# Token mixing of an attention-plus-MLP kernel moved from the second stage into the attention loop

## The chip, the cores and the metric

The kernel runs on one core of one Trainium2 chip. The metric is the device time of one execution in microseconds; the time before is 919.98 us, the median of five runs from 918.11 to 921.35.

In the profile PE is TensorE's matmul and PEld its weight load, DVE is VectorE, ACT is ScalarE, POOL is GpSimd, and SP is the engine that only issues DMAs.

## The reference

Windowed attention with eight global tokens, then a residual MLP with token mixing. Eight batches, eight heads, 576 tokens, 64 numbers per head, 512 per token.

```python
scores = scale * np.matmul(q, k.transpose(0, 1, 3, 2))
mask = np.abs(pos[:, None] - pos[None, :]) <= window          # window = 32
mask = mask | is_global[:, None] | is_global[None, :]
attn = softmax(np.where(mask, scores, -1e9))
x = heads_joined(np.matmul(attn, v))                          # (8, 576, 512)

a1 = alpha1 * x + beta1
tok = np.einsum('ts,bsd->btd', w_tok, a1)                     # token mixing
u = x + lam * tok
a2 = alpha2 * u + beta2
ch = np.maximum(a2 @ w_ch1, 0.0) @ w_ch2                      # 512 -> 2048 -> 512
return u + lam * ch
```

## The kernel before

A prologue loads and folds the weights: W1 and W2 (bf16, with alpha2 and lam inside), wtT, which is w_tok transposed, LA1 = alpha1 * lam and LB1 = beta1 * lam.

**Attention (L270 to L397)** loops over batches and, within each, over heads. Per head the tokens are the rows of q, k and v in five tiles of 128. TensorE transposes q and k into `trps`; VectorE copies them to `QT` and `KT`. `scps` takes the scores of nine 128 x 128 blocks of the band and of the global rows (L335, L340), ScalarE writes their Exp to `PT` (L351), VectorE multiplies `PT` by the mask (L352), and TensorE multiplies with v into `pvps` (L358, L363) and, for the global rows, into `scps` (L372). The 65th column of v is one, so the denominator comes out beside the result. VectorE copies `pvps` to `xstg` (L381, L383) and the denominator of the global rows to `xg` (L385). `vg_ext` (L329, L330) holds v of the global tokens for the head; the score matmuls write the same PSUM tile that it is read from and start behind it. PSUM tiles `scps`, `pvps` and `trps` have one buffer each; SBUF tiles have two. The transposes and copies of q and k run two heads ahead.

At a batch's end SP writes `xstg` to `x_dram` in DRAM (L390), and POOL adds the global rows there with an indirect DMA (L391).

**MLP (L407 to L464)** loops over batches. `X` is read from `x_dram`; VectorE divides it by the denominators (`rden`, L412, L415), makes `XL` = X * LA1 in bf16 (L418) and sets one extra row of it to LB1 (L419). For each of five token tiles, five matmuls of 512 columns with `wtT` make `tkps` (L427), and VectorE adds X to get `U` (L434). Four f32 transposes per tile (L441) go through `utps` to `UT` in bf16 (L442). Then come 128 matmuls of 288 columns into `hps` (L450), each four followed by a Relu on ScalarE into `HT` (L453), and 80 of 512 columns into `chps` (L459). VectorE adds U (L463), and SP stores the result (L464).

The order on each engine is set by a scheduler from priorities in the order of the code, and each engine runs its own list in order. SP issues all loads and stores but those of v and the indirect ones, which POOL issues; a DMA that waits holds up what stands behind it.

Of the kernel before, what the change touches and what calls it, by code (L numbers as in the profile page):

```python
# [67 lines left out]
def kernel(  # L68
# [144 lines left out]
    with tc.tile_pool(name="w_psum", bufs=1, space=bass.MemoryType.PSUM) as wpp:  # L213
        bps = wpp.tile([P, 16], FP32, name="bps")
        for ec in range(16):
            for cc in range(4):
# [33 lines left out]
        nc.vector.tensor_copy(out=wtT[64:65, 4, :], in_=rps[64:65, :])  # L250
    p0_cm.__exit__(None, None, None)

    with (
        tc.tile_pool(name="pG", bufs=2) as pG,
        tc.tile_pool(name="pStage", bufs=2) as pStage,
        tc.tile_pool(name="pA", bufs=2) as pA,
        tc.tile_pool(name="psA_sc", bufs=1, space=bass.MemoryType.PSUM) as psA_sc,
        tc.tile_pool(name="psA_pv", bufs=1, space=bass.MemoryType.PSUM) as psA_pv,
        tc.tile_pool(name="psA_tr", bufs=1, space=bass.MemoryType.PSUM) as psA_tr,
    ):  # L260
# [138 lines left out]
    with (
        tc.tile_pool(name="pB", bufs=2) as pB,  # L400
        tc.tile_pool(name="pBh", bufs=1) as pBh,
        tc.tile_pool(name="psB_tok", bufs=2, space=bass.MemoryType.PSUM) as psB_tok,
        tc.tile_pool(name="psB_h", bufs=2, space=bass.MemoryType.PSUM) as psB_h,
        tc.tile_pool(name="psB_ch", bufs=2, space=bass.MemoryType.PSUM) as psB_ch,
        tc.tile_pool(name="psB_tr", bufs=1, space=bass.MemoryType.PSUM) as psB_tr,
    ):
        for b in range(NBATCH):  # L407
            xd = x_dram[b]
            X = pB.tile([P, NT, XW], FP32, name="X")
            nc.sync.dma_start(out=X, in_=xd.rearrange("(t p) f -> p t f", p=P))  # L410
            rden = pB.tile([P, NT, 8], FP32, name="rden")
            nc.vector.reciprocal(out=rden, in_=X[:, :, DM:XW])  # L412
            rden_b = bass.AP(rden.tensor, rden.offset, [rden.ap[0], rden.ap[1], [1, 8], [0, 64]])
            Xn = X[:, :, 0:DM]
            nc.vector.tensor_tensor(out=Xn, in0=Xn, in1=rden_b, op=ALU.mult)  # L415
            XL = pB.tile([P, NT, DM], BF16, name="XL")
            LA1_b = bass.AP(LA1.tensor, LA1.offset, [LA1.ap[0], [0, NT], [1, DM]])
            nc.vector.tensor_tensor(out=XL, in0=Xn, in1=LA1_b, op=ALU.mult)  # L418
            nc.vector.tensor_copy(out=XL[64:65, 4, :], in_=LB1[64:65, :])  # L419

            U = pB.tile([P, NT, DM], FP32, name="U")
            for t in range(NT):
                tsz = P if t < 4 else 64
                tkps = psB_tok.tile([P, DM], FP32, name="tkps")
                for sc in range(NT):
                    ssz = P if sc < 4 else 65
                    nc.tensor.matmul(  # L427
                        out=tkps[0:tsz, :],
                        lhsT=wtT[0:ssz, sc, t * P : t * P + tsz],
                        rhs=XL[0:ssz, sc, :],  # L430
                        start=(sc == 0),
                        stop=(sc == 4),
                    )
                nc.vector.tensor_tensor(out=U[0:tsz, t, :], in0=tkps[0:tsz, :], in1=Xn[0:tsz, t, :], op=ALU.add)  # L434

            UT = pBh.tile([P, 4, S], BF16, name="UT")
            for t in range(NT):
                tsz = P if t < 4 else 64
                utps = psB_tr.tile([P, 4, P], FP32, name="utps")
                for cc in range(4):  # L440
                    nc.tensor.transpose(out=utps[:, cc, 0:tsz], in_=U[0:tsz, t, cc * P : (cc + 1) * P], identity=ident[0:tsz, 0:tsz])  # L441
                nc.vector.tensor_copy(out=UT[:, :, t * P : t * P + tsz], in_=utps[:, :, 0:tsz])  # L442

            HT = pBh.tile([P, 16, S], BF16, name="HT")
            for ec in range(16):
                for nn in range(2):
                    tsl = slice(0, 288) if nn == 0 else slice(288, S)
                    hps = psB_h.tile([P, 288], FP32, name="hps")
# [46 lines left out]
```

## Time and profile before

| | |
|---|---|
| median of five runs | 919.98 us |
| the profiled execution | 920.4 us |
| its span, first to last instruction | 918.6 us |
| granted TensorE clock, mean | 0.995 |
| TensorE busy | 725.5 us, 79% |
| VectorE busy | 347.5 us, 38% |
| ScalarE busy | 332.1 us, 36% |
| GpSimd busy | 155.5 us, 17% |
| DMA, mean | 90 GB/s |
| end of the attention stage | about 549 us |

Busy shares are means over stages with different limits, so the rows below go stage by stage. A timeline row gives where the instruction starts in the span and how long it ran; in brackets stands how long its engine was idle before it, and what ended that. PE rows overlap, since matmuls are pipelined; how far apart they start tells more than how long one is.

### The profile page before, as it was taken

Reading aid. Unit: us, or ns where it says so; the run is one execution under the profiler, and the core shown is the slowest. Engines: PE = TensorE matmul, PEld = TensorE weight load, DVE = VectorE, ACT = ScalarE, POOL = GpSimd, SP = SyncE. Lnnn points to the kernel's source line nnn. Section 1 sums busy time; section 2 is a strip of 40 time slices with the busy share of each in tenths; the row PEclk is TensorE's granted clock in tenths of the full one; section 3 lists DMA queues with packets and bytes.
Section 4 is the critical chain, followed back from the end, with each engine's and each line's share of the span. In section 5 each row is a group of like instructions: output and inputs, shape, how many; then the busy total and the mean of one; then the engine's idle time right before and its main releaser. Section 6 shows DMA issues by size and latency. Waiting matters only on the chain.

```text
span 918.6 us, 13166 instructions
## 1 busy us (share of the span) xinstructions
PE 725.5 (79%) x5054; PEld 448.2 (49%) x5091; DVE 347.5 (38%) x857; ACT 332.1 (36%) x641; POOL 155.5 (17%) x295
## 2 busy tenths in 40 slices
PE   0158777777777777777777761999999999999988
PEld 0125545545455455454554530556565656556554
DVE  2654333343334343334333324715243352613111
ACT  0014444434344444444444430334260615244251
POOL 0036233242332422422323200000000000000000
PEclk9999999999999999999999999999999999999989
DMA  4826343353433433434334104112113020200101
GB/s 133 342 70 151 90 136 90 88 139 84 126 103 82 136 90 87 139 89 135 90 88 134 39 16 159 59 47 64 55 57 110 12 99 24 87 35 18 46 6 52
DMA packets 114503, 82.83 MB, mean 90 GB/s; under 512 B 90248, under 2 KB 90776, under 8 KB 113928
## 3 DMA queue, kind: packets, MB, share of 16 engines
q1 hardware_dynamic: 106232, 62.60, 23.2%
q0 software_dynamic: 8208, 19.40, 7.1%
q8 instruction: 40, 0.66, 0.3%
q14 instruction: 23, 0.19, 0.1%
HBM read 61.75 MB, written 20.22 MB: 89 GB/s over the span
## 4 chain that ended last, share of the span: by engine, by line
PE 72%; DVE 15%; DMA 7%; issue 3%; ACT 2%; SPq 0%; POOL 0%; POOLq 0%; DVEq 0%
PE chps L459 15%; PE hps L450 14%; PE scps L335 8%; PE pvps L363 8%; PE trps L320 5%; PE trps L317 5%; PE pvps L358 5%; PE tkps L427 3%; DVE QT L318 3%; PE pvps L348 3%; DVE KT L321 3%; DMA w2raw<-in_moe_w_ch_dram 3%; DVE xstg L381 3%; DMA X<-xdram 2%; PE pvps L347 2%
## 5 line engine op out<-in xcount | busy, mean ns | idle before, releaser
L453 ACT ACTIVATE HT<-hps,bias1T 128x288 bf16<-128x288 f32 x256 | 127.2, 501 | 224.5 <-PE hps L450 224.5
L459 PE MATMUL chps<-W,HT 128*128 128x512 bf16 (+1 forms) x611 | 152.0, 380 | 1.1 <-ACT HT L453 0.4
L450 PE MATMUL hps<-UT,W 128*128 128x288 bf16 x1024 | 149.1, 286 | 2.1 <-DVE UT L442 0.2
L450 PEld LDWEIGHTS <-W 128*128 128x128 bf16 x1024 | 99.7, 97 | 46.1 <-issue 21.0
L463 DVE TENSOR_TENSOR ob<-chps,U 128x512 f32<-128x512 f32 (+1 forms) x40 | 27.6, 690 | 203.0 <-PE chps L459 176.9
L351 ACT ACTIVATE PT<-scps 128x1192 f16<-128x1192 f32 x64 | 74.5, 1164 | 64.0 <-PE scps L340 64.0
L305 ACT CAST vext<-vn 128x320 f16<-128x320 f32 x64 | 29.3, 458 | 179.2 <-PE scps L372 177.9
L335 PE MATMUL scps<-QT,KT 64*128 64x128 bf16 x576 | 78.3, 285 | 19.0 <-DVE vg_ext L330 18.4
L459 PEld LDWEIGHTS <-HT 128*128 128x128 bf16 (+1 forms) x640 | 62.1, 100 | 63.4 <-issue 3.4
L358 PE MATMUL pvps<-vg_ext,pgc 8*128 8x65 f16 x320 | 73.9, 231 | 0.0
L317 PE MATMUL trps<-identb,qn 128*64 128x128 bf16 x320 | 44.6, 304 | 33.8 <-DVE KT L321 30.9
L363 PE MATMUL pvps<-voext,PT 128*128 128x65 f16 x448 | 71.1, 240 | 0.0
L427 PE MATMUL tkps<-XL,wtT 128*128 128x512 bf16 (+2 forms) x192 | 52.4, 394 | 23.3 <-DVE XL L418 21.5
L381 DVE COPY xstg<-pvps 128x320 f32<-128x320 f32 x64 | 31.5, 492 | 95.0 <-PE pvps L363 95.0
L320 PE MATMUL trps<-identb,kn 128*64 128x128 bf16 x320 | 44.5, 302 | 25.3 <-DVE QT L318 25.3
L318 DVE COPY QT<-trps 64x640 bf16<-64x640 bf16 x64 | 30.9, 483 | 85.1 <-PE scps L340 79.7
L264 POOL DMA_DIRECT2D vn<-in_v_dram x63 | 58.1, 922 | 28.2 <-ACT xg L384 24.1
L340 PE MATMUL scps<-qgT,KT 64*128 64x8 bf16 x320 | 62.5, 211 | 0.0
L317 PEld LDWEIGHTS <-qn 128*64 128x64 bf16 x320 | 39.2, 166 | 42.4 <-issue 42.0
L363 PEld LDWEIGHTS <-PT 128*128 128x128 f16 x576 | 40.7, 111 | 36.9 <-DVE PT L352 19.3
L335 PEld LDWEIGHTS <-KT 64*128 64x128 bf16 x576 | 55.4, 127 | 1.4 <-issue 1.4
L340 PEld LDWEIGHTS <-KT 64*128 64x128 bf16 x320 | 41.4, 129 | 28.2 <-issue 28.2
(94 smaller groups left out, 823.4 us busy)
## 6 DMA issues: line engine op xcount, KB each, us to landing
xdram<-xstg SPq DMA_DIRECT2D x8, 1300.0 KB
X<-xdram SPq DMA_DIRECT2D x8, 1300.0 KB
qn<-in_q_dram SPq DMA_DIRECT2D x63, 160.0 KB
kn<-in_k_dram SPq DMA_DIRECT2D x63, 160.0 KB
vn<-in_v_dram POOLq DMA_DIRECT2D x63, 160.0 KB
vo<-in_v_dram POOLq DMA_DIRECT2D x64, 128.0 KB
out_dram<-ob SPq DMA_DIRECT2D x32, 256.0 KB
w1raw<-in_moe_w_ch_dram SPq DMA_DIRECT2D x1, 4096.0 KB
```

Source lines behind the costliest of these rows:

```text
L317: nc.tensor.transpose(out=trps[:, c, :], in_=qn16[:, c, :], identity=identb)
L320: nc.tensor.transpose(out=trps[:, c, :], in_=kn16[:, c, :], identity=identb)
L335: nc.tensor.matmul(out=scps[:, bi * P : (bi + 1) * P], lhsT=KTf[:, c : c + P], rhs=QT[:, t, :], start=True, stop=True)
L340: nc.tensor.matmul(out=scps[:, GR_OFF + 8 * si : GR_OFF + 8 * si + 8], lhsT=KTf[:, c : c + P], rhs=qgT[:, 8 * h : 8 * h + 8], start=True, ...
L351: nc.scalar.activation(out=PT, in_=scps[:, 0:SCORE_F], func=AF.Exp, bias=0.0, scale=0.125)
L358: nc.tensor.matmul(out=pvps[:, t * PV_T : t * PV_T + PV_T], lhsT=pgc[:, gsl], rhs=vg_ext, start=True, stop=False)
L363: nc.tensor.matmul(out=pvps[:, t * PV_T : t * PV_T + PV_T], lhsT=PT[:, bi * P : (bi + 1) * P], rhs=rhs, start=False, stop=(ci == len(tbis) ...
L381: nc.vector.tensor_copy(out=xstg[:, :, D * h : D * h + D], in_=src_num)
L427: nc.tensor.matmul(out=tkps[0:tsz, :], lhsT=wtT[0:ssz, sc, t * P : t * P + tsz], rhs=XL[0:ssz, sc, :], start=(sc == 0), stop=(sc == 4),)
L450: nc.tensor.matmul(out=hps, lhsT=W1[:, cc, ec * P : (ec + 1) * P], rhs=UT[:, cc, tsl], start=(cc == 0), stop=(cc == 3))
L453: nc.scalar.activation(out=HT[:, ec, tsl], in_=hps, func=AF.Relu, bias=bias1T[:, ec : ec + 1], scale=1.0)
L459: nc.tensor.matmul(out=chps[0:tsz, :], lhsT=HT[:, ec, t * P : t * P + tsz], rhs=W2[:, ec, :], start=(ec == 0), stop=(ec == 15))
```

## The change

The token mixing, from the load of X to UT, leaves the MLP loop and becomes `emit_B1(batch, piece)`, eight pieces:
- piece 0 loads X and takes the reciprocal `rden`;
- piece 1 multiplies X by it and, new, runs two f32 matmuls of 512 columns (`warm`) whose result nobody reads;
- piece 2 makes XL and clears half a tile of U;
- pieces 3 to 7 each make one `tkps` and one tile of U; the last of them also transposes all of U to UT and writes U and UT to DRAM (`u_dram`, `ut_dram`).

Within head h of batch b the code now calls `emit_B1(b - 1, h)`; batch 7's eight pieces follow the loop. The MLP loop reads U and UT back from DRAM and starts with hps. `tkps` has one PSUM buffer instead of two. HT and UT get pools that are open from before the attention on.

```diff
+        def emit_B1(bb, piece):
+            if bb < 0:
+                return
+            st = b1st
+            if piece == 0:
+                st["X"] = pB1.tile([P, NT, XW], FP32, name="X")
+                nc.sync.dma_start(out=st["X"], in_=x_dram[bb].rearrange("(t p) f -> p t f", p=P))
+                st["rden"] = pB1.tile([P, NT, 8], FP32, name="rden")
+                nc.vector.reciprocal(out=st["rden"], in_=st["X"][:, :, DM:XW])
+            elif piece == 1:
...
+                nc.vector.tensor_tensor(out=st["X"][:, :, 0:DM], in0=st["X"][:, :, 0:DM], in1=rden_b, op=ALU.mult)
+                warm = psB_tok.tile([P, DM], FP32, name="warm", tag="tkps")
+                for _w in range(2):
+                    nc.tensor.matmul(out=warm, lhsT=ident, rhs=st["X"][:, _w, 0:DM], start=True, stop=True)
+            elif piece == 2:
...
+                nc.vector.tensor_tensor(out=st["XL"], in0=st["X"][:, :, 0:DM], in1=LA1_b, op=ALU.mult)
+                nc.vector.tensor_copy(out=st["XL"][64:65, 4, :], in_=LB1[64:65, :])
+                st["U"] = pB1.tile([P, NT, DM], FP32, name="U")
+                nc.vector.memset(st["U"][64:P, 4, :], 0.0)
+            elif piece <= 7:
+                t = piece - 3
...
+                nc.vector.tensor_tensor(out=st["U"][0:tsz, t, :], in0=tkps[0:tsz, :], in1=st["X"][0:tsz, t, 0:DM], op=ALU.add)
+                if t == 4:
...
+                    nc.sync.dma_start(out=u_dram[bb], in_=st["U"].rearrange("p t c -> p (t c)"))
+                    nc.sync.dma_start(out=ut_dram[bb], in_=UT.rearrange("p c s -> p (c s)"))
...
             for h in range(H):
+                emit_B1(b - 1, h)
...
+        for piece in range(8):
+            emit_B1(NBATCH - 1, piece)
...
+            UT = pCu.tile([P, 4, S], BF16, name="UT2")
+            nc.sync.dma_start(out=UT, in_=ut_dram[b])
+            U = pC.tile([P, NT, DM], FP32, name="U")
+            nc.sync.dma_start(out=U, in_=u_dram[b])
```

How the order moves, at three places. VectorE, third head of batch 1, from the mask multiply to the vg_ext cast of the next head, before:

```order
L352 TENSOR_TENSOR PT<-PT,mask 128x1192
L302 CAST qn_1750<-qn 128x320
L381 COPY xstg<-pvps 128x5x64
L383 TENSOR_SCALAR xstg<-pvps 128x5
L385 TENSOR_SCALAR xg<-scps 8x1
L329 CAST vg_ext<-scps 8x64
L330 MEMSET vg_ext 8x1
```

The same place now (L411 is the mask multiply, L440 the copy, L388 the cast):

```order
L411 TENSOR_TENSOR PT<-PT,mask 128x1192
L278 RECIPROCAL rden<-X 128x40
L361 CAST qn_1759<-qn 128x320
L281 TENSOR_TENSOR X<-X,rden 128x5x512
L440 COPY xstg<-pvps 128x5x64
L288 TENSOR_TENSOR XL<-X,LA_180 128x2560
L442 TENSOR_SCALAR xstg<-pvps 128x5
L289 CAST XL<-LB_182 1x512
L444 TENSOR_SCALAR xg<-scps 8x1
L305 TENSOR_TENSOR U<-tkps,X 128x512
L388 CAST vg_ext<-scps 8x64
L389 MEMSET vg_ext 8x1
```

Five instructions of the token mixing stand between the seven. In batches 4 to 7 the order is the same; in batches 2 and 3 rden and the multiplies stand behind the copy.

SP, batches 1 and 2, with tile numbers; before, only loads and the store of xstg:

```order
L390 DMA xdram0_60<-xstg_374 128x5x520
L264 DMA kn_1559<-in_k_dram 128x5x64
L264 DMA qn_1641<-in_q_dram 128x5x64
L264 DMA kn_1642<-in_k_dram 128x5x64
L264 DMA qn_1744<-in_q_dram 128x5x64
```

Now, from the store of xstg on (L449; X is the token mixing's load):

```order
L449 DMA xdram0_60<-xstg_405 128x5x520
L322 DMA kn_1631<-in_k_dram 128x5x64
L322 DMA qn_1753<-in_q_dram 128x5x64
L276 DMA X_1091<-xdram0_60 128x5x520
L322 DMA kn_1754<-in_k_dram 128x5x64
```

The load of X stands between the loads of k and q, and seven loads later the stores of U and UT do; five loads behind those stands the MLP's own load of UT (`UT_6533<-utdram_348`).

TensorE, from the last attention matmul on, before:

```order
L372 MATMUL scps<-voext,PT 8x65
L372 LDWEIGHTS PT
L372 MATMUL scps<-voext,PT 8x65
L427 LDWEIGHTS wtT
L427 MATMUL tkps<-XL,wtT 128x512
```

The same place now (L431 is the attention matmul, L477 the first of the MLP's 128):

```order
L431 MATMUL scps<-voext,PT 8x65
L431 LDWEIGHTS PT
L431 MATMUL scps<-voext,PT 8x65
L477 LDWEIGHTS W_192
L477 MATMUL hps<-UT_6533,W_192 128x288
```

hps has taken the place of tkps. Batch 7's warm matmuls stand 122 matmuls further on (109 hps, 13 chps), and its tkps and utps behind those, between hps and chps of batch 0.

## Rows read from the trace of the kernel before

**Rows 1.** By stretch: length, busy PE, PEld, DVE, ACT, POOL, granted clock, DMA.

```profile
77.00:544.00 467.00, 362.32 (x2863) 234.10 (x2860) 181.98 (x576) 195.42 (x368) 138.06 (x266) 1.00 0.38 101
620.00:918.60 298.60, 288.93 (x1724) 171.43 (x1753) 96.66 (x123) 111.31 (x224) 0.00 (x0) 0.99 0.15 51
570.50:576.00 5.50, 5.26 (x13) 2.01 (x15) 5.44 (x5) 0.00 (x0) 0.00 (x0) 1.00 0.00 0
```

**Rows 2.** Timeline, one head: start, us long, engine, line [idle before].

```profile
300.41 0.49 DVE L381 COPY xstg<-pvps 128x320 f32<-128x320 f32 x1 [1.45 <-PE pvps L363]
...
302.22 0.26 PE L335 MATMUL scps<-QT,KT 64*128 64x128 bf16 x1 [0.30 <-DVE vg_ext L330]
...
303.51 1.17 ACT L351 ACTIVATE PT<-scps 128x1192 f16<-128x1192 f32 x1 [1.00 <-PE scps L340]
...
305.15 0.76 DVE L352 TENSOR_TENSOR PT<-PT,mask 128x1192 f16<-128x1192 f16 x1
...
306.01 0.33 DVE L302 CAST qn<-qn 128x320 bf16<-128x320 f32 x1
...
307.79 0.49 DVE L381 COPY xstg<-pvps 128x320 f32<-128x320 f32 x1 [1.45 <-PE pvps L363]
```

**Rows 3.** Timeline at the hand-over of the stages.

```profile
549.33 0.15 DVE L385 TENSOR_SCALAR xg<-scps 8x1 f32<-8x1 f32 x1
...
564.77 2.83 DVE L415 TENSOR_TENSOR X<-X,rden 128x2560 f32<-128x2560 f32 x1
...
570.51 0.61 PE L427 MATMUL tkps<-XL,wtT 128*128 128x512 bf16 x1 [21.46 <-DVE XL L418]
...
571.34 5.10 PE L427 MATMUL tkps<-XL,wtT 128*128 128x512 bf16 x13 [0.22 <-issue]
```

**Rows 4.** Chain of waits, same place: start, us, what.

```profile
549.32 4.96 DMA xdram<-xstg
555.13 2.93 DMA xdram<-xg,gsc
558.19 5.83 DMA X<-xdram
```

**Rows 5.** Timeline of the MLP stage.

```profile
619.69 2.23 PE L427 MATMUL tkps<-XL,wtT 128*128 128x512 bf16 x9 [0.16 <-issue]
...
622.34 1.25 PE L427 MATMUL tkps<-XL,wtT 128*128 128x512 bf16 x5
...
623.86 1.25 PE L427 MATMUL tkps<-XL,wtT 128*128 128x512 bf16 x5
...
871.13 1.25 PE L427 MATMUL tkps<-XL,wtT 128*64 128x512 bf16 x5
...
873.74 0.66 PE L441 MATMUL utps<-ident,U 128*128 128x128 f32 x4 [0.79 <-DVE UT L442]
...
900.33 14.10 PE L459 MATMUL chps<-W,HT 128*128 128x512 bf16 x63
```

**Rows 6.** Groups by line: form xcount | busy us, mean ns | idle.

```profile
L264 POOL DMA_DIRECT2D vn<-in_v_dram x63 | 58.1, 922 | 28.2 <-ACT xg L384 24.1 <-ACT voext L310 4.1
...
L434 DVE TENSOR_TENSOR U<-tkps,X 128x512 f32<-128x512 f32 (+1 forms) x40 | 27.4, 688 | 11.3 <-PE tkps L427 11.3
...
L442 DVE CAST UT<-utps 128x512 bf16<-128x512 f32 (+1 forms) x40 | 24.8, 621 | 5.0 <-PE utps L441 5.0
...
L418 DVE TENSOR_TENSOR XL<-X,LA 128x2560 bf16<-128x2560 f32 x8 | 22.5, 2817 | 0.0
L415 DVE TENSOR_TENSOR X<-X,rden 128x2560 f32<-128x2560 f32 x8 | 22.5, 2815 | 0.1
...
L419 DVE CAST XL<-LB 1x512 bf16<-1x512 f32 x8 | 3.3, 418 | 0.3
L412 DVE RECIPROCAL rden<-X 128x40 f32<-128x40 f32 x8 | 3.2, 402 | 18.9 <-DMA X<-xdram 18.9
```

**Rows 7.** POOL's add of the global rows in batch 1.

```profile
136.46 1.41 POOL L391 DMA_INDIRECT xdram<-xg,gsc  x1 [0.78 <-DVE xg L385]
```

More of the change, by code (lines that the diff above doesn't have):

```diff
@@ L251 @@
     p0_cm.__exit__(None, None, None)
+    u_dram = [dramp.tile([P, NT * DM], FP32, name=f"udram{b}") for b in range(NBATCH)]
+    ut_dram = [dramp.tile([P, 4 * S], BF16, name=f"utdram{b}") for b in range(NBATCH)]
+    pCu = ctx.enter_context(tc.tile_pool(name="pCu", bufs=2))
+    pCh = ctx.enter_context(tc.tile_pool(name="pCh", bufs=1))
     with (
@@ L256 @@
         tc.tile_pool(name="pA", bufs=2) as pA,
+        tc.tile_pool(name="pB1", bufs=2) as pB1,
         tc.tile_pool(name="psA_sc", bufs=1, space=bass.MemoryType.PSUM) as psA_sc,
@@ L259 @@
         tc.tile_pool(name="psA_tr", bufs=1, space=bass.MemoryType.PSUM) as psA_tr,
-    ):
+        tc.tile_pool(name="psB_tok", bufs=1, space=bass.MemoryType.PSUM) as psB_tok,
+        tc.tile_pool(name="psB_tr", bufs=1, space=bass.MemoryType.PSUM) as psB_tr,
+    ):
+        b1st = {}
+        def emit_B1(bb, piece):
[8 more added lines that the diff above has]
+            elif piece == 1:
+                rden_b = bass.AP(st["rden"].tensor, st["rden"].offset, [st["rden"].ap[0], st["rden"].ap[1], [1, 8], [0, 64]])
+                nc.vector.tensor_tensor(out=st["X"][:, :, 0:DM], in0=st["X"][:, :, 0:DM], in1=rden_b, op=ALU.mult)
[3 more added lines that the diff above has]
+            elif piece == 2:
+                st["XL"] = pB1.tile([P, NT, DM], BF16, name="XL")
+                LA1_b = bass.AP(LA1.tensor, LA1.offset, [LA1.ap[0], [0, NT], [1, DM]])
+                nc.vector.tensor_tensor(out=st["XL"], in0=st["X"][:, :, 0:DM], in1=LA1_b, op=ALU.mult)
[4 more added lines that the diff above has]
+                t = piece - 3
+                tsz = P if t < 4 else 64
+                tkps = psB_tok.tile([P, DM], FP32, name="tkps")
+                for sc in range(NT):
+                    ssz = P if sc < 4 else 65
+                    nc.tensor.matmul(
+                        out=tkps[0:tsz, :],
+                        lhsT=wtT[0:ssz, sc, t * P : t * P + tsz],
+                        rhs=st["XL"][0:ssz, sc, :],
+                        start=(sc == 0),
+                        stop=(sc == 4),
+                    )
+                nc.vector.tensor_tensor(out=st["U"][0:tsz, t, :], in0=tkps[0:tsz, :], in1=st["X"][0:tsz, t, 0:DM], op=ALU.add)
+                if t == 4:
+                    UT = pB1.tile([P, 4, S], BF16, name="UT")
+                    for tt in range(NT):
+                        tsz2 = P if tt < 4 else 64
+                        utps = psB_tr.tile([P, 4, P], FP32, name="utps")
+                        for cc in range(4):
+                            nc.tensor.transpose(
+                                out=utps[:, cc, 0:tsz2], in_=st["U"][0:tsz2, tt, cc * P : (cc + 1) * P], identity=ident[0:tsz2, 0:tsz2]
+                            )
+                        nc.vector.tensor_copy(out=UT[:, :, tt * P : tt * P + tsz2], in_=utps[:, :, 0:tsz2])
+                    nc.sync.dma_start(out=u_dram[bb], in_=st["U"].rearrange("p t c -> p (t c)"))
+                    nc.sync.dma_start(out=ut_dram[bb], in_=UT.rearrange("p c s -> p (c s)"))
@@ L397 @@
             )
+        for piece in range(8):
+            emit_B1(NBATCH - 1, piece)
     with (
[L400 to L405, printed above, removed]
+        tc.tile_pool(name="pC", bufs=2) as pC,
@@ L406 @@
+        tc.tile_pool(name="psC_h", bufs=2, space=bass.MemoryType.PSUM) as psC_h,
+        tc.tile_pool(name="psC_ch", bufs=2, space=bass.MemoryType.PSUM) as psC_ch,
     ):
         for b in range(NBATCH):
[L408 to L444, printed above, removed]
+            UT = pCu.tile([P, 4, S], BF16, name="UT2")
@@ L447 @@
                     tsl = slice(0, 288) if nn == 0 else slice(288, S)
-                    hps = psB_h.tile([P, 288], FP32, name="hps")
+                    hps = psC_h.tile([P, 288], FP32, name="hps")
                     for cc in range(4):
@@ L456 @@
                 tsz = P if t < 4 else 64
-                chps = psB_ch.tile([P, DM], FP32, name="chps")
+                chps = psC_ch.tile([P, DM], FP32, name="chps")
                 for ec in range(16):
```

3 lines of the change are left out of this document (2 added, 1 removed).

## Prediction

> **What bounds the kernel now.** I read, in this order, the table by stage, one head's timeline, the hand-over between the two stages with the chain of waits there, the MLP stage's timeline, and the groups by line.
>
> The table by stage [rows 1]: in the attention stage (77 to 544 us) TensorE is busy 362 of 467 us and VectorE 182; in the MLP stage (620 to the end) TensorE is busy 289 of 299 us. The granted clock is 1.00, which is 2.4 GHz, in the first and 0.99 in the second. So attention is bound by a chain and not by one engine, and the MLP stage by TensorE.
>
> One head [rows 2]: the copy of pvps to xstg starts at 300.41 and, for the next head, at 307.79: 7.38 us. In between run, one behind the other, the copy, the xg add and the vg_ext cast on VectorE, the score matmuls (from 302.22, 1.81 behind the copy), the Exp (303.51), the mask multiply (305.15 to 305.91, so it ends 5.50 behind the copy), the PV matmuls, and the next copy. VectorE stands in this chain several times. It has one long free stretch, the 1.45 us ahead of the copy. Any other VectorE work that is queued in front of the copy, the vg_ext cast or the mask multiply makes the head longer.
>
> The hand-over [rows 3, 4]: the last xg add ends at 549.33 + 0.15 = 549.48. Then xstg goes to DRAM, the global rows are added, X is read back, two multiplies of 2.82 us run, and TensorE, idle for 21.46 us, starts at 570.51. Thirteen of its next tkps matmuls take 5.10 us, where five of the same shape take 1.25 later [rows 5].
>
> The MLP stage [rows 5]: the tkps of one batch start at 619.69 and those of the sixth batch after it at 871.13: 41.91 us per batch.
>
> **Part 1: the end of the program, a saving.** Before, from 549.48 to the end of the span, 918.6: 369.1 us. After:
> - hps stands right behind the last attention matmul in TensorE's order, and its UT comes from DRAM, loaded heads earlier (both in the listings of the change). Start: 0.2 us.
> - What stays per batch is hps and chps. A group of five tkps with its four utps transposes takes 623.86 - 622.34 = 1.52 us [rows 5]; five groups make 7.6, and 41.9 - 7.6 = 34.3. Eight batches: 274.4.
> - Batch 7 has no head left to run beside. Its 7.6 us of tkps and utps go between hps and chps, and two warm matmuls (f32, 512 columns) with them. The trace has no such matmul. Bounds: the bf16 matmul of 512 columns, 1.25 / 5 = 0.25 each, so 0.5; and four f32 transposes of 128 columns, 0.66 [rows 5], each, so 1.3. I take 1.0, nearer to the f32 row.
> - Batch 7's X chain is as long as before: the multiply by rden ends at 564.77 + 2.83 = 567.6 [rows 3], 18.1 us behind 549.48. In TensorE's order 109 hps and 13 chps stand ahead of warm. 64 chps take 14.3, by 63 in 14.10 [rows 5], so sixteen rounds of eight hps and one chps take 34.3 - 14.3 = 20.0, 1.25 each, and 13.5 rounds 16.9: TensorE is idle for 1.2. Its waits for U and UT were up to 0.79 in the last batch [rows 5] and now have hps and chps between them: 1.3. Together 2.5.
> - From the last chps (900.33 + 14.10 = 914.43) to the end: 4.2.
>
> 0.2 + 274.4 + 7.6 + 1.0 + 2.5 + 4.2 = 289.9; saved, **79.2 us**.
>
> I cost the reloads of U and UT at nothing here: they are issued about a batch (34 us) ahead, and X, of the same size as U, lands in 5.83 [rows 4]. Without that cover TensorE would wait some 6 us per batch.
>
> **Part 2: attention, a loss.** Batches 1 to 7 take in the token mixing of the batch before. On VectorE that is 0.40 + 2.82 + 2.82 + 0.42 + 5 x 0.69 + 5 x 0.62 = 13.0 us per batch [rows 6], 13.3 with a memset of some 0.3. What counts is where these stand in VectorE's order: the pieces are written over eight heads, but are queued within about three.
>
> *Batches 1, 4, 5, 6, 7.* Behind the third head's mask multiply stand rden, the qn cast and the multiply by rden: 5.50 + 0.40 + 0.33 + 2.82, less 0.3 of overlap, is 8.7 instead of 7.38, so the copy is 1.3 late. Behind the copy come XL (2.82) and the LB cast (0.42), then tkps' fifth matmul, the U add (0.69), and only then vg_ext: scores start 5.5 behind the copy instead of 1.81, 3.7 late. The next two hand-overs lose 1.2 together: four tkps and up to four utps stand ahead of PV on TensorE, of which the mask multiply covers all but 0.4 each time, and a U add ahead of vg_ext costs 0.2. In the fourth head of the row the mask multiply stands ahead of the KT copy, as long as the QT copy, 0.48: 0.5 back. With 0.1 of remainders: **5.8 us**.
>
> *Batches 2 and 3.* The copy comes on time, but rden and both multiplies stand between it and vg_ext: 5.5. Later hand-overs: 0.6. **6.1 us**.
>
> 5 x 5.8 + 2 x 6.1 = **41.2 us**, less than half of 7 x 13.3 = 93. TensorE's added 7.6 us per batch lie, but for the 0.4 above, in its waits (105 us idle of 467 [rows 1]).
>
> **Queues.** X's load stands on SP until the global rows have landed. POOL starts their add at 136.46 [rows 7]; 2.93 later [rows 4] X can go, and 5.83 after that it is there: about 145.4. rden's turn comes 7.38 + 5.50 behind the copy of batch 1's first head, and that copy is about a us ahead of POOL's start: 148. So there is no wait, with some 2.6 us in hand. The qn and kn loads behind X on SP have nearly two heads until their casts. The memset of U waits for the write of the U that had its buffer; by the order that write is issued one head ahead, some 7.6 us, and takes 5 like xstg's 4.96 [rows 4].
>
> **Sum.** Span: 918.6 - 79.2 + 41.2 = 880.6. The profiled execution took 920.4, 1.8 over its span and 0.4 over the median of 919.98: 880.6 + 1.8 = **882 us**.
>
> **Rivals.**
> - *Nothing is hidden* (slower than before). If all added VectorE work lay on the chain, attention would lose 93: 882 + 93 - 41 = 934. It turns slower from 79.2 / 7 = 11.3 us per batch. For it: VectorE runs in order and is in the chain. Against: it is idle for 61% of attention [rows 1]. 4%.
> - *Late transfers.* The 2.6 us in hand for X, or for U's write, go to the traffic of kn, qn, vn and vo; then VectorE's whole queue waits. 3 us in each of seven batches: 903. 12%.
> - *POOL in the way.* POOL issues vn and vo just behind the copy, 0.92 us for vn [rows 6] and as much, I take it, for vo, where XL now runs. If XL waited for all of it, 1.8 x 7 = 13: 895. 10%. The Trainium skill (GPSIMD Engine Reference, Key points) says that GpSimd shares its SBUF interfaces with VectorE and contends with VectorE instructions that have two SBUF inputs, as XL has. No row here shows such an overlap: both large multiplies ran with POOL idle.
> - *The clock.* The slow matmuls of 571.34 come back in the stretched hand-overs. One head's score and PV matmuls (1.3 + 1.9 us by [rows 2]) at half rate: 3.2 x 7 = 22: 904. Against: the longest wait that I find for TensorE is under 2.5 us, and the warm matmuls lie in it. 4%. The Trainium skill (TensorE: Matmul & The Clock Gate, What's actually happening) says that an idle array falls back to half its clock until work releases it; the slow matmuls behind the 21.46 us agree, the granted clock of that stretch, 1.00 [rows 1], does not show it.
> - *hps waits for batch 7 after all* (the change doesn't do what it says): the 21.5 us come back, 904. The order speaks against it. 2%.
> - *More is hidden than I count*, 3 us per batch: 861. 6%.
>
> **How the numbers follow.** The forecast has the other 62%; its own range is 872 to 892, 1.4 us per batch either way. The range that holds 8 in 10 takes in POOL and the late transfers above, and 4 us under the forecast's own range below: 868 to 904. A measurement of this kernel tells 0.2%, 2 us. Slower: 0.04, the first rival; within 0.2%: 0.01; faster: 0.95.
>
> **What would show it.** Right: the first hps starts within 1 us of the last attention matmul, at about 590 in the profile; TensorE then has no wait of over 2 us; in batches 1, 4, 5, 6 and 7 two heads take about 8.7 and 11.5 us from copy to copy, in 2 and 3 one takes 12.9, and the other heads stay within 0.7 of 7.38; rden has no wait for X. Wrong: rden or the memset idle behind a DMA; XL longer than 2.82 us; tkps ahead of the first hps; unchanged heads that take longer than 7.38.

## The result and the profile after

The changed kernel takes 877.93 us (median of eight runs, 876.56 to 879.26), the kernel before 920.48 (median of fifteen): a ratio of 0.9543, 95% interval 0.9532 to 0.9554. The ratios are estimated from the fast runs and not from two medians; one of the fifteen runs took 1070.95 us and stands apart. The medians are 42.5 us apart; the forecast was 882, which is 38 below the 919.98 that it started from. The profiled execution took 876.8 us, its span 875.0.

The head of its page: the first line is the span, then busy time by engine, then two rows of the 40 slices, PE's busy tenths and the granted clock (9 is 90% or more).

```profile
span 875.0 us, 13279 instructions
PE 721.1 (82%) x5076; PEld 432.9 (49%) x5123; DVE 347.1 (40%) x865; ACT 331.6 (38%) x641; POOL 155.2 (18%) x295
PE   0158777977977977977977977979999999999998
PEclk9999999955865865955955955959999999999999
```

TensorE and VectorE are about as busy as before (725.5 and 347.5 us); the saving is idle time. The hole of slice 25 is gone. The granted clock is new: 0.5 to 0.6 in most of attention, with a 9 or 8 once per batch, where the page of before has 9 throughout.

**Where the saving is.** The end of attention, and the first rows of the MLP stage behind it (timelines of VectorE and TensorE: start, us long):

```profile
585.24 0.15 DVE L444 TENSOR_SCALAR xg<-scps 8x1 f32<-8x1 f32 x1
585.44 3.04 PE L477 MATMUL hps<-UT,W 128*128 128x288 bf16 x12 [0.47 <-DVE xg L444]
...
599.81 0.40 DVE L278 RECIPROCAL rden<-X 128x40 f32<-128x40 f32 x1 [14.42 <-DMA X<-xdram]
600.25 2.83 DVE L281 TENSOR_TENSOR X<-X,rden 128x2560 f32<-128x2560 f32 x1
603.11 2.82 DVE L288 TENSOR_TENSOR XL<-X,LA 128x2560 bf16<-128x2560 f32 x1
604.37 1.94 PE L284 MATMUL warm<-X,ident 128*128 128x512 f32 x4
```

Attention ends at 585.39, against 549.48 before [rows 3]: 35.9 us longer, forecast 41.2. hps starts 0.05 us behind it, where before TensorE stood idle for 21.46 us [rows 3, 4], and the chain of batch 7's X runs beside hps. From 585.39 to the end of the span it is 289.6 us, forecast 289.9. So the tail gave 369.1 - 289.6 = 79.5 back, and attention took 35.9.

**The big hand-over of batch 1** on VectorE and TensorE, to be read beside [rows 2]:

```profile
147.82 0.39 DVE L278 RECIPROCAL rden<-X 128x40 f32<-128x40 f32 x1
148.14 0.25 DVE L361 CAST qn<-qn 128x320 bf16<-128x320 f32 x1
148.31 2.80 DVE L281 TENSOR_TENSOR X<-X,rden 128x2560 f32<-128x2560 f32 x1
151.04 0.47 DVE L440 COPY xstg<-pvps 128x320 f32<-128x320 f32 x1
151.44 2.80 DVE L288 TENSOR_TENSOR XL<-X,LA 128x2560 bf16<-128x2560 f32 x1
...
157.08 0.69 DVE L305 TENSOR_TENSOR U<-tkps,X 128x512 f32<-128x512 f32 x1 [2.13 <-PE tkps L298]
157.69 0.20 DVE L388 CAST vg_ext<-scps 8x64 f16<-8x64 f32 x1
...
151.17 3.78 PE L284 MATMUL warm<-X,ident 128*128 128x512 f32 x4 [1.07 <-DVE X L281]
155.01 0.58 PE L298 MATMUL tkps<-XL,wtT 128*128 128x512 bf16 x1
155.82 1.23 PE L298 MATMUL tkps<-XL,wtT 128*128 128x512 bf16 x3 [0.22 <-issue]
157.18 0.38 PE L407 MATMUL pvps<-QT,kgT 64*8 64x512 bf16 x1
```

The order is the one the prediction walked through, and rden does not wait for X. Two things differ. The warm matmuls take 3.78 us here, 1.94 in batch 7, and outlast XL; the first tkps takes 0.58, the next three 1.23 together. TensorE is slow at first, and fast from about 156.6, where the record of the clock has its first rise.

**The clock, told by a matmul's duration.** The pvps matmul of 64 x 512, by form, in the kernel before (300 to 361 us), then in the changed kernel between two bursts of token mixing (184 to 216) and behind one (226 to 242): count, busy us, mean ns.

```profile
L348 PE MATMUL pvps<-QT,kgT 64*8 64x512 bf16 x8 | 5.0, 628 | 0.0
...
L407 PE MATMUL pvps<-QT,kgT 64*8 64x512 bf16 x4 | 2.5, 629 | 0.0
...
L407 PE MATMUL pvps<-QT,kgT 64*8 64x512 bf16 x2 | 0.8, 376 | 0.0
```

And windows of the changed kernel, three in batch 1 and then the two stretches of the matmul above (length; busy us of PE, PEld, DVE, ACT, POOL; granted clock; DMA):

```profile
162.00:170.00 8.00, 7.84 (x69) 4.61 (x69) 5.72 (x14) 3.18 (x6) 1.82 (x4) 1.00 0.36 93
170.00:177.00 7.00, 6.13 (x65) 4.21 (x65) 4.73 (x13) 3.07 (x6) 1.82 (x4) 1.00 0.57 212
177.00:184.00 7.00, 5.17 (x43) 3.21 (x42) 3.07 (x9) 3.18 (x6) 1.85 (x4) 0.51 0.81 241
184.00:216.00 32.00, 25.07 (x201) 16.33 (x199) 12.60 (x41) 12.73 (x24) 11.73 (x20) 0.50 0.63 189
226.00:242.00 16.00, 15.34 (x136) 9.10 (x134) 10.86 (x27) 7.53 (x13) 3.64 (x8) 1.00 0.36 101
```

The same matmul takes 629 ns at a granted clock of 0.50, which is 1.2 GHz, and 376 ns at 1.00, which is 2.4 GHz. In the attention of the kernel before it took 628: that stage ran at 1.2 GHz, though [rows 1] show 1.00 there. The record of the clock has no entry ahead of its first change, and in the kernel before that comes only at the hand-over of the stages, at 575.6 us. The Trainium skill (TensorE: Matmul & The Clock Gate, Seeing it yourself) warns against trusting every recorded clock event and wants a cross-check. Here the recorded entries fit the durations; what misleads is the stretch ahead of the first one.

Heads, from the start of one pvps copy to the next, in us (the kernel before: 7.38, and 8.86 where the batch changes):

```
changed kernel   head 1    2     3     4     5     6     7    (8: batch change)
batch 1          7.38  8.64 12.09  7.64  6.72  6.96  7.69  8.85
batch 2          7.38  7.39 13.90  6.81  7.15  7.07  7.37  8.86
batch 4          7.38  8.64 11.06  7.64  7.06  6.96  7.69  8.85
```

Behind the burst two or three heads are clearly shorter than 7.38. The fifth of batch 1 (170.77 to 177.49) and the fourth and fifth of batch 2 have a granted clock of 1.00. The sixth of batch 1 (6.96, from 177.49 on) has 0.50: there VectorE's mask multiply stands ahead of the KT copy and starts 4.30 behind the head's first copy, where it was 4.74 before [rows 2]. So not every short head is the clock's.

### The profile page after: what moved, and what is told of

Its sections match the earlier page's. It is cut to its first block, busy times and chain, and to the rows that moved or that the text cites. A ratio compares the mean times of both kernels' runs of the same rounds, so it can differ in the third digit from the quotient of the medians.

```text
span 875.0 us, 13279 instructions
## 1 busy us (share of the span) xinstructions
PE 721.1 (82%) x5076; PEld 432.9 (49%) x5123; DVE 347.1 (40%) x865; ACT 331.6 (38%) x641; POOL 155.2 (18%) x295
## 4 chain that ended last, share of the span: by engine, by line
PE 74%; DVE 14%; DMA 5%; issue 3%; ACT 3%; SPq 0%; POOL 0%; ACTq 0%; DVEq 0%
PE chps L486 15%; PE hps L477 14%; PE scps L394 7%; PE pvps L422 7%; PE tkps L298 6%; PE pvps L417 4%; PE trps L379 4%; PE trps L376 4%; DMA w2raw<-in_moe_w_ch_dram 3%; PE pvps L407 3%; PE utps L312 2%; PE warm L284 2%; DVE QT L377 2%; DVE X L281 2%; ACT HT L480 2%
## 5 line engine op out<-in xcount | busy, mean ns | idle before, releaser
L477 PE MATMUL hps<-UT,W 128*128 128x288 bf16 x1024 | 154.5, 288 | 3.4 <-ACT HT L480 1.4
L477 PEld LDWEIGHTS <-W 128*128 128x128 bf16 x1024 | 99.2, 97 | 49.8 <-issue 6.9
L394 PE MATMUL scps<-QT,KT 64*128 64x128 bf16 x576 | 68.3, 261 | 12.1 <-DVE vg_ext L389 11.5
L413 ACT ACTIVATE pgc<-pvps 8x640 f16<-8x640 f32 x64 | 44.3, 692 | 66.7 <-PE pvps L407 66.6
L422 PE MATMUL pvps<-voext,PT 128*128 128x65 f16 x448 | 67.6, 229 | 0.0
L365 POOL MEMSET vext<- 128x5 f16 x64 | 7.9, 123 | 315.0 <-PE scps L431 314.9
L440 DVE COPY xstg<-pvps 128x320 f32<-128x320 f32 x64 | 31.4, 490 | 75.7 <-PE pvps L422 75.7
L376 PE MATMUL trps<-identb,qn 128*64 128x128 bf16 x320 | 41.2, 279 | 22.5 <-DVE KT L380 19.6
L298 PE MATMUL tkps<-XL,wtT 128*128 128x512 bf16 (+3 forms) x185 | 54.5, 397 | 3.6 <-issue 1.7
L399 PE MATMUL scps<-qgT,KT 64*128 64x8 bf16 x320 | 56.1, 195 | 0.0
L379 PE MATMUL trps<-identb,kn 128*64 128x128 bf16 x320 | 39.4, 275 | 16.9 <-DVE QT L377 16.1
L411 DVE TENSOR_TENSOR PT<-PT,mask 128x1192 f16<-128x1192 f16 x64 | 48.9, 764 | 11.2 <-ACT PT L410 11.2
```

Of the source, the lines that this page charges most:

```text
L298: nc.tensor.matmul(out=tkps[0:tsz, :], lhsT=wtT[0:ssz, sc, t * P : t * P + tsz], rhs=st["XL"][0:ssz, sc, :], start=(sc == 0), stop=(sc == 4),)
L376: nc.tensor.transpose(out=trps[:, c, :], in_=qn16[:, c, :], identity=identb)
L379: nc.tensor.transpose(out=trps[:, c, :], in_=kn16[:, c, :], identity=identb)
L394: nc.tensor.matmul(out=scps[:, bi * P : (bi + 1) * P], lhsT=KTf[:, c : c + P], rhs=QT[:, t, :], start=True, stop=True)
L399: nc.tensor.matmul(out=scps[:, GR_OFF + 8 * si : GR_OFF + 8 * si + 8], lhsT=KTf[:, c : c + P], rhs=qgT[:, 8 * h : 8 * h + 8], start=True, ...
L422: nc.tensor.matmul(out=pvps[:, t * PV_T : t * PV_T + PV_T], lhsT=PT[:, bi * P : (bi + 1) * P], rhs=rhs, start=False, stop=(ci == len(tbis) ...
```

## The experiments

All edits are to the changed kernel unless said otherwise. The questions were: what the two warm matmuls do, whether the stretch of attention is VectorE's in-order queue, as the prediction has it, and what the clock has to do with it.

### Without the warm matmuls

```diff
-                warm = psB_tok.tile([P, DM], FP32, name="warm", tag="tkps")
-                for _w in range(2):
-                    nc.tensor.matmul(out=warm, lhsT=ident, rhs=st["X"][:, _w, 0:DM], start=True, stop=True)
```

> The two f32 matmuls (warm) are left out; the output does not change. Theory 'they cost': in batch 1 of the changed kernel they take 3.78 us at the 1.2 GHz level and end some 0.7 us after XL, so the first tkps is 0.7 us late; 0.7 x 7 = 5, so 873 against 877.9, and the third head of batch 1 falls from 12.09 to 11.4. Theory 'they raise the clock': TensorE runs at 2.4 GHz for some 20 us behind each batch's tkps, where heads take 6.7 to 7.1 instead of 7.4, and the warm matmuls are what brings that; without them some 2 us per batch come back, 14 in all, so 878 - 5 + 14 = 887. Neither: 877.9, within 1.

Measured: 900.74 us (892.38 to 902.08), ratio to before 0.9769 (0.9738 to 0.9800). That is 22.8 more than with them, beyond the 14 of the second theory. TensorE in batch 1:

```profile
155.13 2.29 PE L295 MATMUL tkps<-XL,wtT 128*128 128x512 bf16 x5 [4.20 <-DVE XL L285]
157.61 0.63 PE L404 MATMUL pvps<-QT,kgT 64*8 64x512 bf16 x1
160.06 1.89 PE L295 MATMUL tkps<-XL,wtT 128*128 128x512 bf16 x4
163.46 1.91 PE L295 MATMUL tkps<-XL,wtT 128*128 128x512 bf16 x4
168.31 0.38 PE L404 MATMUL pvps<-QT,kgT 64*8 64x512 bf16 x1
```

TensorE is idle for 4.20 us until XL is there and then does three groups of tkps at 1.2 GHz; it is fast at 168.31, not at 157.18. The third head takes 14.91 instead of 12.09, and in batches 3 and 4 the fourth takes over 10.6. Two matmuls whose result nobody reads are worth half of the 42.5 us that the change saves.

### Six added matmuls in every head

To the kernel before, and then to the changed kernel, in each head:

```diff
+                dmy = psA_d.tile([P, DM], FP32, name="dmy")
+                for _d in range(3):
+                    nc.tensor.matmul(out=dmy, lhsT=qn16[:, 0:2, :], rhs=W1[:, _d, 0:DM], start=True, stop=True)
                 PT = pA.tile([P, SCORE_F], FP16, name="PT")
...
+                dmy = psA_d.tile([P, DM], FP32, name="dmy")
+                for _d in range(3):
+                    nc.tensor.matmul(out=dmy, lhsT=PT[:, 0:P], rhs=PT[:, 0:DM], start=True, stop=True)
                 src_num = bass.AP(pvps.tensor, pvps.offset, [pvps.ap[0], [PV_T, NT], [1, D]])
```

> The kernel before with six added matmuls of 512 columns per head whose result nobody reads, three ahead of the next scores and three behind PV. Theory 'attention of the kernel before ran at the 1.2 GHz level': the added matmuls lift it, the pvps matmul of 512 columns falls from 0.63 to 0.38 us, a head falls from 7.38 to between 6.7 and 7.1 as behind the tkps of the changed kernel, and 64 heads x 0.3 to 0.6 make 19 to 38 us: 882 to 901 against 920.5. Rival 'it ran at 2.4 GHz, as the page's 1.00 says': matmul durations stay, and the added 6 x 0.25 = 1.5 us per head cost between nothing and 96 us: 920 to 1016.

Measured: 1026.16 us, ratio 1.1159 (1.1138 to 1.1181). The added matmuls don't lift the clock for good. Its page (granted clock), two windows, and the group of the first three added matmuls:

```profile
PEclk9999985555555555555555555569999999999999
146.00:217.00 71.00, 66.76 (x397) 32.70 (x396) 22.90 (x72) 23.53 (x47) 16.89 (x34) 0.50 0.29 78
217.00:221.00 4.00, 2.46 (x28) 1.54 (x28) 1.40 (x5) 2.16 (x3) 2.26 (x3) 0.93 1.03 274
L353 PE MATMUL dmy<-W,qn 128*128 128x512 bf16 x192 | 103.7, 616 | 0.0
```

Here the record has its first entry at 142 us, at the end of batch 0, and from there to 681 it says 0.5, but for three short rises at changes of batch (142 to 146, 217 to 221, 439 to 443). A matmul of 512 columns takes 616 ns, against 380 for those of chps on the same page. So the first half of the theory, that attention of the kernel before runs at 1.2 GHz, stands; the second half, that these matmuls lift it, fell. The rival named a price up to 1016 for the added work and came nearer to the time, though it denied the low level.

> The changed kernel with the same six added matmuls per head. Theory 'the clock': the heads away from the tkps, about 5 of 8 in batches 1 to 7 and all of batch 0, 43 in all, gain 0.3 to 0.6 each, 13 to 26 us, and the slow warm matmuls (3.78 us) become fast ones (1.94), up to 0.7 x 6 = 4 more: 848 to 865 against 877.9. Rival 'no gain, TensorE only gets more work': 878 to 970.

Measured: 924.26 us, ratio 1.0051 (1.0033 to 1.0068), 46 more than the changed kernel: within the rival's range, and the gain of the first theory didn't come. Heads of batch 1: 9.25, 9.24, 10.90, 8.84, 6.96, 6.95, 7.86. Away from the token mixing a head takes 9.24, as in the run above; behind it, at a granted clock of 1.00, a head with the same six matmuls takes 6.96. So the added work is hidden at one level and costs 1.86 us per head (9.24 - 7.38) at the other: at 1.2 GHz TensorE has no room for the six within a head, at 2.4 it has.

### XL made twice

```diff
                 nc.vector.tensor_tensor(out=st["XL"], in0=st["X"][:, :, 0:DM], in1=LA1_b, op=ALU.mult)
+                nc.vector.tensor_tensor(out=st["XL"], in0=st["X"][:, :, 0:DM], in1=LA1_b, op=ALU.mult)
```

> The changed kernel with the multiply that makes XL done twice, one behind the other (2.8 us more on VectorE per batch). Theory 'the stretch of attention is VectorE's in-order queue, with XL between the copy and vg_ext': each of seven batches loses 2.8 more, 20 us, and the tail between 0 and 2.8: 898 to 901. Rival 'transfers, POOL or TensorE's added work set the stretch': VectorE has room, 878 to 881.

Measured: 911.58 us (two runs, 909.67 and 913.49), ratio 0.9908 (0.9880 to 0.9936). Beyond both theories: 33.7 us more than the changed kernel, 14 over VectorE's own 2.8 x 7 = 20. The next run says why.

```diff
-                for _w in range(2):
-                    nc.tensor.matmul(out=warm, lhsT=ident, rhs=st["X"][:, _w, 0:DM], start=True, stop=True)
+                for _w in range(4):
+                    nc.tensor.matmul(out=warm, lhsT=ident, rhs=st["X"][:, _w, 0:DM], start=True, stop=True)
```

> The changed kernel with XL made twice, as in the run before (911.6, which was 33.7 us and not 20 over the changed kernel), and with four warm matmuls instead of two, so that TensorE has work until the second XL ends. Theory 'the surplus of 14 us is TensorE's clock: it stood idle for the second XL and began the tkps at 1.2 GHz': the surplus goes, VectorE's 2.8 x 7 = 20 stay, and five tkps at 2.4 GHz from the start give back up to 1 per batch: 891 to 899. Theory 'the surplus is more VectorE queueing': four warm matmuls change nothing or add to it: 909 to 920.

Measured: 894.42 us, ratio 0.9709 (0.9687 to 0.9731), 17 us less with more work, and within the first theory's range. TensorE in batch 4, first with two warm matmuls, then with four:

```profile
357.58 3.78 PE L284 MATMUL warm<-X,ident 128*128 128x512 f32 x4 [1.06 <-DVE X L281]
363.58 2.32 PE L299 MATMUL tkps<-XL,wtT 128*128 128x512 bf16 x5 [1.59 <-DVE xg L445]
368.54 1.89 PE L299 MATMUL tkps<-XL,wtT 128*128 128x512 bf16 x4
```

```profile
356.19 5.49 PE L284 MATMUL warm<-X,ident 128*128 128x512 f32 x8 [1.06 <-DVE X L281]
362.19 1.25 PE L299 MATMUL tkps<-XL,wtT 128*128 128x512 bf16 x4
365.38 1.04 PE L299 MATMUL tkps<-XL,wtT 128*128 128x512 bf16 x4
```

With two, TensorE waits again before XL is done and begins the tkps at the low level (batches 5 to 7 are alike; in 1 to 3 the level rises within the warm matmuls and falls again before or within the first five tkps); with four the level rises within the warm matmuls, and tkps run at the high level from the first. The third head of batch 4 takes 11.06 us in the changed kernel, 17.40 with XL twice, 13.47 with XL twice and four warm matmuls. So 2.4 of the 6.3 go to VectorE's queue, close to the 2.8 added, and 3.9 to the clock. Over batches 1 to 7, from copy to copy, the second XL costs 33.5 us with two warm matmuls and 16.4 with four, 1.4 to 3.7 in a batch. The split is not exact: four warm matmuls without the second XL were not run.

### VectorE's small steps taken out of the way of the scores

vg_ext is made once per batch for all heads, and the two denominator copies run on ScalarE, without their + 1e-9. First on the kernel before:

```diff
+            vg_all = pG.tile([8, H, PV_T], FP16, name="vg_all")
+            nc.vector.tensor_copy(out=vg_all[:, :, 0:D], in_=gps_t[0:8, 512:1024].rearrange("p (h d) -> p h d", h=H))
...
-                nc.vector.tensor_copy(out=vg_ext[:, 0:D], in_=scps[0:8, SC_VG : SC_VG + 64])
...
-                nc.vector.tensor_scalar(out=xstg[:, :, DM + h : DM + h + 1], in0=src_den, scalar1=1e-9, scalar2=None, op0=ALU.add)
+                nc.scalar.copy(out=xstg[:, :, DM + h : DM + h + 1], in_=src_den)
```

> The kernel before, with VectorE's small steps taken out of the way of the scores: vg_ext is made for all eight heads at a batch's start, and the two denominator copies (to xstg and xg) run on ScalarE, without their + 1e-9. Scores then wait for the copy of pvps and for ScalarE alone. In the kernel before they start 1.81 us behind the start of that copy, which takes 0.49; 0.5 to 1.0 us per head should go, 32 to 64 us in all: 856 to 888 against 920. It is the base for the next run.

Measured: 858.48 us, ratio 0.9331 (0.9315 to 0.9347). A head takes 6.12 instead of 7.38, a change of batch 9.88 instead of 8.86: the chain through VectorE that [rows 2] show is real.

> The changed kernel with the same edit, so that XL, which still stands behind the copy on VectorE, no longer stands ahead of what the scores wait for. Theory 'the stretch at the big hand-over is VectorE's queue ahead of vg_ext': beside what the edit brings to the kernel before, the 3.7 us per batch that scores came late shrink by 2 to 3.5, 14 to 24 us in seven batches; so the gain of the change, 42.5 us between the plain kernels, grows to 57 to 67 between these two. Theory 'TensorE's added work at the 1.2 GHz level sets the stretch': with scores between them the tkps follow less closely, TensorE rises to 2.4 GHz later, as without the warm matmuls (900.7), and the gain of the change shrinks to 20 to 42.

Measured: 838.09 us, ratio 0.9132 (0.9098 to 0.9166). The gain of the change between these two kernels is 20.4 us, not 57 to 67: the theory of the queue fell in this form, and the second one's 20 to 42 held at its edge. Two batches say why, the first two rows batch 1, the others batch 2:

```profile
145.18 3.78 PE L284 MATMUL warm<-X,ident 128*128 128x512 f32 x4
152.41 2.31 PE L298 MATMUL tkps<-XL,wtT 128*128 128x512 bf16 x5
...
216.78 3.29 PE L284 MATMUL warm<-X,ident 128*128 128x512 f32 x4
221.40 1.04 PE L298 MATMUL tkps<-XL,wtT 128*128 128x512 bf16 x4
```

In batch 2 the warm matmuls end faster than they began, and the tkps run at the high level; heads 3 to 7 take 7.43, 7.94, 6.24, 6.00 and 6.89, 3.9 us over five plain heads. In batch 1 they don't; attention's own matmuls stand between them and the tkps, and heads 3 to 7 take 9.63, 10.74, 9.93, 8.70 and 6.73: 15.1 over. Batch 6 is like batch 1, 17.2 over. With VectorE out of the way, TensorE's added work at 1.2 GHz is what is late next.

### Three ways to bring the rise ahead

The multiply by rden in two parts, and three warm matmuls that wait for the first of them alone:

```diff
-                nc.vector.tensor_tensor(out=st["X"][:, :, 0:DM], in0=st["X"][:, :, 0:DM], in1=rden_b, op=ALU.mult)
+                for t0, t1 in ((0, 2), (2, NT)):
+                    rd = st["rden"][:, t0:t1, :]
+                    rden_b = bass.AP(rd.tensor, rd.offset, [rd.ap[0], rd.ap[1], [1, 8], [0, 64]])
+                    nc.vector.tensor_tensor(out=st["X"][:, t0:t1, 0:DM], in0=st["X"][:, t0:t1, 0:DM], in1=rden_b, op=ALU.mult)
...
-                for _w in range(2):
+                for _w in (0, 1, 0):
```

> The changed kernel with the multiply by rden in two parts (two token tiles, then three) and three f32 warm matmuls that wait for the first part alone, so they can follow PV without the idle 1.07 us. Theory 'what counts is that TensorE works without a gap until tkps': the rise comes ahead of the first tkps instead of within it, tkps start at most 0.5 us later and five of them take 1.1 to 1.3 us instead of 1.8 to 2.2; 0.5 to 1.5 us per batch, 4 to 10 us: 868 to 874 against 877.9. Theory 'the added matmuls only stand in the way' (they outlast XL): 1 us or more per batch, 885 or above.

Measured: 880.43 us (875.01 to 887.40), ratio 0.9564 (0.9496 to 0.9631): neither, and inconclusive as a time. The mechanism works, since the five tkps behind take 1.24 us. Batch 5, the last row a window:

```profile
411.68 4.75 PE L286 MATMUL warm<-X,ident 128*128 128x512 f32 x6
416.49 1.24 PE L300 MATMUL tkps<-XL,wtT 128*128 128x512 bf16 x5
427.94 1.89 PE L300 MATMUL tkps<-XL,wtT 128*128 128x512 bf16 x4
...
424.00:428.00 4.00, 4.00 (x31) 2.37 (x31) 2.40 (x9) 1.65 (x5) 1.82 (x4) 0.72 0.23 74
```

and the third head of batch 1 falls from 12.09 to 10.61. But in three batches (5 to 7) the level falls within the token mixing, as the third row shows, and the fourth head takes 10.63 instead of 7.64. In the traced execution (884.42) batches 1 and 2 win 1.8 us and batches 5 to 7 lose 7.6.

Three warm matmuls instead of two in the kernel of 838.1:

```diff
-                for _w in range(2):
+                for _w in range(3):
```

> The changed kernel with VectorE's small steps out of the way of the scores, as in the run before (838.1), and with three warm matmuls instead of two. There the batches in which the clock rose within the warm matmuls lost 4 to 6 us, and the two in which it did not (1 and 6) 15 and 17. Theory 'it is the clock': with a longer stretch without a gap fewer batches miss the rise; against 1 to 1.9 us more work in each of seven batches stands 11 us in one or two: 822 to 836. Theory 'the added matmuls only stand in the way': 843 to 851.

Measured: 816.40 us (815.15 to 817.61), ratio 0.8873 (0.8855 to 0.8891), under the range given: the fastest version. In batch 1 the rise now comes within the warm matmuls:

```profile
145.09 4.42 PE L284 MATMUL warm<-X,ident 128*128 128x512 f32 x6
150.93 1.29 PE L298 MATMUL tkps<-XL,wtT 128*128 128x512 bf16 x4
```

Six of these records take 4.42 us where four took 3.78. Batch 1 loses 3.8 us instead of 15.1, batch 6 6.0 instead of 17.2, 22.5 together; the two medians are 21.7 apart, the two traced executions 18.9 (spans 832.3 and 813.4; the first is the fastest run of its kernel). Against the kernel before with the same edit (858.5) the change is now worth 42.1.

That is no more than the 42.5 between the plain kernels. From the first copy of batch 1 to the last of batch 7 the token mixing costs 34.8 us here and 36.0 in the changed kernel. VectorE no longer stands ahead of the scores, but in TensorE's own order the warm matmuls now stand between the scores and the pvps matmuls behind them. Batch 3:

```profile
263.31 5.04 PE L284 MATMUL warm<-X,ident 128*128 128x512 f32 x6
268.29 0.22 PE L410 MATMUL pvps<-QT,kgT 64*8 64x128 bf16 x1
```

So the forecast that the loss shrinks once vg_ext is out of the queue fell even where the rise comes in every batch.

tkps and utps in two shared PSUM buffers, with two warm matmuls:

```diff
-        tc.tile_pool(name="psB_tok", bufs=1, space=bass.MemoryType.PSUM) as psB_tok,
-        tc.tile_pool(name="psB_tr", bufs=1, space=bass.MemoryType.PSUM) as psB_tr,
+        tc.tile_pool(name="psB_tok", bufs=2, space=bass.MemoryType.PSUM) as psB_tok,
...
-                        utps = psB_tr.tile([P, 4, P], FP32, name="utps")
+                        utps = psB_tok.tile([P, 4, P], FP32, name="utps", tag="tkps")
```

> The same kernel as of the 838.1 run, with two warm matmuls, but tkps and utps share two PSUM buffers instead of having one each, so that ten tkps matmuls can follow one another. Theory 'it is the clock': the longer stretch without a gap makes TensorE rise in every batch by the end of the second group, and batches 1 and 6 lose 6 to 9 instead of 15 and 17: 820 to 832. Rival 'the blocks of tkps ahead of scores cost more than the clock brings': 840 to 860.

Measured: 839.76 us, ratio 0.9139 (0.9107 to 0.9171): no gain. Batches 1 and 6 lose 8.3 and 9.7 us, as the theory had it, but batch 4 loses 8.2 (9.16, 9.76, 5.70, 5.62, 8.60 for heads 3 to 7) where it lost 5.9. In batch 4 the level rises within the warm matmuls and falls again as the block of tkps begins, which stands ahead of attention's matmuls:

```profile
333.06 4.02 PE L297 MATMUL tkps<-XL,wtT 128*128 128x512 bf16 x9
```

Only in batches 2 and 3 do all tkps of the first block run at the high level.

## Why the prediction was right, and where it was not

**The tail: right.** 289.6 us against 289.9. hps follows attention at once (0.05 us), batch 7's X chain ends its multiply 17.7 us behind the last xg add (603.08 - 585.39; 18.1 was taken), and the reloads of U and UT are hidden: from 590 to 632 us TensorE is busy 41.78 of 42. Two small terms were off and nearly cancel: warm took 1.94 us instead of 1.0, and TensorE has no gap of the kind for which 2.5 were taken, none over 0.44. From batch 0's first hps to batch 1's it takes 45.89, 11.7 more than from batch 1's to batch 2's (34.17), for which 7.6 + 1.0 + 2.5 = 11.1 were forecast.

```profile
590.00:632.00 42.00, 41.78 (x242) 24.07 (x245) 15.97 (x19) 14.42 (x29) 1.47 (x1) 1.00 0.47 180
```

**The stretch of attention: 35.9 instead of 41.2, the term that was mis-sized.** In batches 1 and 4 to 7 the two late heads were forecast at 8.7 and 11.5 us and took 8.64 or 8.65 and 11.06 to 12.35. "The next two hand-overs lose 1.2 together" is the step that failed: batch 1's fourth and fifth head take 7.64 + 6.72 = 14.36, 0.4 under two plain heads, with TensorE at 2.4 GHz. How much of that is the clock is shown by the run with early warm matmuls: where the level falls there, the fourth head takes 10.63. In batches 2 and 3 the big hand-over took 13.90 and 13.37 instead of 12.9, and the heads behind it, forecast 0.6 longer, were 1.1 and 1.6 shorter (28.40 and 27.96 against 4 x 7.38 = 29.52). One of them, 6.61 in batch 3, left the 0.7 around 7.38 that the prediction allowed. The "0.5 back" of the mask multiply is there: the sixth head's 6.96 at 0.50, of which the seventh, 7.69, gives 0.3 up again.

**The clock: wrong at the root.** "The granted clock is 1.00, which is 2.4 GHz" was read from [rows 1] for attention. The matmul durations of the same trace say 1.2 GHz, and the run with added matmuls in every head shows 0.50 recorded for a matmul that is as slow. The rival of the clock had the sign reversed: it asked what a fall would cost in a stage that was already at the low level. What was there to be had was a rise. The Trainium skill (TensorE: Matmul & The Clock Gate, What's actually happening) says that the throttled state is the default and that work releases it; the rise within the warm matmuls and the tkps agrees with that.

**The warm matmuls: a step that was missing.** They were costed at 1.0 us in the tail and at nothing in attention. They bring the rise ahead of most of the tkps, and without them the change saves 18.7 us (919.47 - 900.74), not 42.5, and 900.74 lies outside the forecast's own 872 to 892. That the time was hit is in so far luck. The walk through the heads used tkps of 0.25 us, which are those of the 2.4 GHz level; at 1.2 GHz five take 2.3, not 1.25. So it was right on the tkps because of an edit that it gave no value, and wrong on the heads behind them for the same reason.

**VectorE's queue: right as a mechanism, not alone.** XL twice, with TensorE kept at work, cost 2.4 us in batch 4's hand-over, to which it adds 2.8 on VectorE. But a wait on VectorE also cost TensorE its clock: without such work the same 2.8 cost 6.3. And with VectorE's steps out of the way the loss stayed as large, 34.8 us against 36.0, since TensorE's added work took their place.

**POOL in the way: fell.** POOL issues vn and vo beside XL, and XL takes its 2.80 us:

```profile
150.86 0.85 POOL L322 DMA_DIRECT2D vn<-in_v_dram  x1 [0.52 <-ACT xg L443]
151.71 0.76 POOL L367 DMA_DIRECT2D vo<-in_v_dram  x1
```

XL runs from 151.44 to 154.24, and all eight of its kind average 2.81, as before. The contention that the Trainium skill (GPSIMD Engine Reference, Key points) names does not show in this overlap of 1.0 us, in which POOL only issues DMAs.

**Late transfers: fell.** X lands in 6.8 us at the median of its issues, and rden waits for it in batch 7 alone, where it was expected to. The memset of U waits for no DMA.

What stays open: why the level falls again while TensorE goes on working, as in batch 5 of the run with early warm matmuls (busy 4.00 us of those from 424 to 428, where it falls), and why six added matmuls per head raise it only three times, and briefly. The runs show that it is so, not why. The changed kernel with a third warm matmul and nothing else was not run, so what that one is worth without the relief is open too.

## What to carry to other kernels

Read TensorE's level from the duration of one form of matmul at two places, not from the clock column alone, and do it before costing anything on TensorE. Where a chain makes TensorE wait just ahead of a burst, work without a gap that ends with the wait can be worth far more than it costs (22.8 us here), and what lengthens the wait on another engine can cost twice (33.5 us here instead of 16.4). A step that is taken off one engine's queue is worth only what the next engine leaves: VectorE's relief brought 61 us in the kernel before (919.3 to 858.5), 40 in the changed one with two warm matmuls, and 62 together with a third.

## What the runs showed of the hardware that was not expected

- The column of the granted clock shows 1.00 ahead of the first recorded change, whatever the level: 628 ns under 1.00 in the kernel before, 629 under 0.50 and 376 under 1.00 after the first change.
- Attention with six added matmuls of 512 columns per head stayed at 1.2 GHz (616 ns each) but for three short rises, while two f32 matmuls and the tkps behind them brought 2.4 GHz in each of seven batches of the changed kernel.
- One f32 matmul of 512 columns shows as two records; two such matmuls take 3.78 us at 1.2 GHz and 1.94 at 2.4.
- Runs of one kernel differ more where the rise fails in some batches: 875.0 to 887.4 with early warm matmuls, 834.1 to 843.6 with two behind the relieved scores, 815.2 to 817.6 with three, where it came in every batch of the traced run. That the clock makes the difference between two runs is not shown: of the runs with early warm matmuls the longer two have the lower mean granted clock, of those with the relieved scores the longest has not the lowest.
